# Eight products of a retention kernel issued as transpositions, and the first up stage in another order

## The chip, the cores and the metric

The kernel runs on one core of one Trainium2 chip. The time is the device time of one execution, in microseconds (us). The core has a matrix engine (TensorE; PE in the profile, its weight loads PEld), VectorE (DVE), ScalarE (ACT), GpSimd (POOL), and SyncE (SP), which here only issues DMAs. Each engine takes its instructions in the order of the program and stops at the first one whose inputs are not there.

## The reference, cut to what matters

```python
batch, n_heads, seq, head_dim = (4, 8, 768, 64)
for t in range(S):                      # retention, per batch and head
    state = gamma * state + outer(k[t], v[t])
    y[t] = scale * q[t] @ state
x = y.transpose(0, 2, 1, 3).reshape(3072, 512)
n_tokens, d_model, d_ff = (3072, 512, 1536)
g = x @ w_gate                          # feed-forward (SwiGLU)
out = (g * sigmoid(g) * (x @ w_val)) @ w_out
```

The weights arrive as 64-bit floats, q, k and v as 32-bit floats.

## The kernel before, in words

The 3072 tokens are worked through in four segments of 768 tokens, each of six chunks of 128 tokens (three chunks of two batches). A segment has an up stage (products with w_gate and w_val, for 12 blocks f of 128 columns of d_ff) and a down stage (products with w_out). Retention is computed chunk by chunk with a mask of decays inside a chunk and a state carried between chunks. Only the first segment's up stage is touched by the change. It is special in two ways: retention of its own six chunks precedes the products, and the weights are read raw from DRAM, turned to 32-bit floats on ScalarE, VectorE and GpSimd, and written back to DRAM for the later segments.

To keep the precision of 32-bit floats in a fast one-pass format, x and the weights are each split into three parts (a, b, c). A product of a weight block with 384 tokens is 12 matmuls in one bank of PSUM: four each for the parts a, b and c, in this order.

**What sets the order.** The order of nearly all work is a list written out by hand, PLAN (lines 51 to 229). Each token of it calls one step (the table at lines 576 to 597); the order of the tokens is the order of instructions on every engine, and of DMAs on SyncE's queue. A token is a letter and a number n, after a colon a part. The ones that the texts below use:

- Loads, all on SyncE's queue: `A` one of five pieces of the decay tables (A0: half the mask, A1 and A2: the other half, A3: q's decays, A4: k's decays). `ln:w` one operand of chunk n: w = 0 k (laid out with the head dimension on the partitions), 1 q, 2 v, 3 k's second layout (tokens on the partitions). `Un:b`, `Vn:b` the raw weights of block n into raw buffer b (512 KB for w_val and as much for w_gate; for the first block the two halves are loaded separately). `Zn` writes converted weights back to DRAM. Blocks 12 to 17 are the six pairs of rows of w_out.
- Retention of chunk n: `s` scores (matmuls L632, then two VectorE multiplications with the mask, L638). `r` makes k's second layout for chunks 0 and 1, which have no load `l0:3`, `l1:3`: four products on TensorE of 128 columns of k with a unit matrix (L693), left in a bank of PSUM. `K0` and `E1` scale that result by the decays (VectorE L653; ScalarE L660, eight instructions), `k`, `q`, `Q` scale k and q (GpSimd or VectorE). `t` the chunk's contribution to the state (L715), all in bank 6, then added or copied out (ScalarE L718 for chunks 0 and 1, VectorE L720 later). `g` decays the state (ScalarE L701). `o` the part of y from the old state (L730), `m` the part from the scores (L744) and the first part of x (ScalarE L1000). `x` the other two parts of x.
- Conversion of weight block n: `a`, `b`, `c` on ScalarE (L533, L536, L539), `S` on VectorE (L546), `C` on VectorE (L554) or GpSimd (L556, for the first two blocks and for w_out). `T` forms sums of weight blocks for later segments. `c` of block f stands behind the load of block f + 2 into the same raw buffer and waits for it to land.
- Products: `nf:0`, `nf:1`, `nf:2` make the three parts of the w_gate block f on ScalarE (L991), VectorE (L994) and GpSimd (L997); `nf:3` to `nf:5` do so for w_val. `p` and `v` are the products of blocks 0 and 1 for a third of the tokens (L937), `G` and `W` those of the later blocks for half the tokens (L919; G with w_gate, W with w_val). `u`/`i` apply SiLU on ScalarE (L943, L443), `y`/`j` multiply on VectorE (L948, L443). Each of the four banks is used again for the next block: `G` of block f + 1 waits for `i` of block f, `W` for `j`.

The function that the diff touches is `rows_of`; `scale_k` and `scale_k_act` read its result, `state` reads theirs.

Of the kernel before, what the change touches and what calls it, by code (L numbers as in the profile page):

```python
# [17 lines left out]
P = 128  # L18
# [7 lines left out]
L = 3  # L26
# [22 lines left out]


PLAN = """
    A0 l0:0 l1:0 A2 A1 U0:0 I0 l0:2 s0 a0:1 s1 A3 b0:1 c0:1 r0 l2:1 l2:0 A4 S0:1 m0 r1 l2:3 l1:2 K0
    l3:0 s2 l3:1 Q2 V0:0 E1 x0:2 C0:1 n0:0 t0 l2:2 m1 t1 l4:1 a0:0 b0:0 n0:1 s3 S0:0 x0:1 x1:1 c0:0
    k2 l4:0 U1:1 q3 g2 n0:2 o2 C0:0 n0:3 l3:3 o3 g3 a1:1 b1:1 m2 x1:2 l3:2 t2 n0:4 s4 a1:0 l5:0 S1:1
    n0:5 l5:1 b1:0 p0:0 u0:0 l4:2 l5:2 x2:1 v0:0 k3 q4 S1:0 m3 c1:1 t3 s5 y0:0 U2:0 x3:2 q5 x2:2
    c1:0 x3:1 o4 m4 C1:1 T0:0 U12:3 o5 n1:0 C1:0 x4:1 n1:1 m5 p0:1 x5:1 a2 v0:1 n1:3 T0:1 n1:2 u0:1
    b2 n1:4 U3:1 p1:0 h0 T1:0 p1:1 T0:2 y0:1 S2 U4:0 l5:3 a12 x5:2 T1:1 n1:5 u1:0 a3 x4:2 v1:0 Z0
    v1:1 p0:2 y1:0 u1:1 y1:1 c2 C2 v0:2 p1:2 b12 u0:2 v1:2 T1:2 U5:1 n2:0 a4 b3 Z1 n2:1 n2:3 y0:2 S3
    c3 n2:4 n2:2 C3 U6:0 G2:0 u1:2 y1:2 G2:1 T2:0 i2:0 n3:0 S12 n2:5 W2:0 b4 n3:1 W2:1 T2:1 S4 i2:1
    l4:3 U13:2 n3:3 c12 n3:2 T2:2 a5 c4 G3:1 C4 j2:0 c13 n3:4 j2:1 b5 G3:0 U7:1 i3:0 C12 n4:0 Z2  # L60
    n4:3 T3:0 n3:5 Z12 n4:1 S5 W3:0 n4:4 i3:1 c5 a6 n4:2 T3:1 n4:5 a13 W3:1 G4:0 G4:1 C5 b6 n5:0
    j3:1 T4:0 T3:2 T4:1 W4:1 U14:3 n5:3 j3:0 i4:1 n5:1 U8:0 b13 g4 n5:4 S6 W4:0 T4:2 n5:2 c6 Z3 L
    j4:1 i4:0 T5:0 a7 S13 G5:1 C6 n5:5 n6:0 Z4 j4:0 C13 b7 G5:0 n6:1 U9:1 W5:1 n6:3 i5:0 i5:1 c14 S7
    T5:1 T5:2 a8 n6:2 Z5 n6:4 T6:0 W5:0 G6:1 c7 C7 Z13 j5:0 n7:0 n6:5 G6:0 j5:1 b8 W6:1 i6:1 n7:3
    n7:1 U10:0 k4 a14 U15:2 k5 T6:1 n7:2 b14 n7:4 G7:1 S8 i6:0 c8 g5 T6:2 a9 T7:0 S14 W6:0 C8 i7:1
    G7:0 c15 i7:0 j6:1 Z6 T7:1 T7:2 U11:1 j6:0 n8:0 n7:5 n8:3 n8:1 n8:4 C14 n8:2 b9 W7:1 j7:1 Z14 S9
    a10 h1 W7:0 n8:5 c9 G8:0 C9 j7:0 a15 i8:0 Z7 b15 G8:1 n9:0 a11 U16:3 T8:0 S15 n9:1 P1 b10 W8:0
    n9:3 W8:1 S10 c10 t4 C15 n9:2 n9:4 C10 c16 G9:0 i8:1 T9:0 n9:5 Z15 b11 a16 i9:0 G9:1 j8:1 U17:2
    S11 t5 T9:1 n10:0 W9:1 h2 j8:0 b16 n10:1 T8:1 S16 W9:0 i9:1 T8:2 P0 n10:3 j9:1 n10:2 C16 G10:0
    j9:0 n10:4 P2 c11 i10:0 1/was0.0 G10:1 Z16 C11 n10:5 T10:0 T9:2 Z8 0/h0.0 n11:0 0/h0.1 W10:0  # L70
    n11:3 a17 n11:4 W10:1 1/sc0 T11:0 T11:1 Z9 i10:1 0/W0 1/begin n11:1 T11:2 Z11 0/h0.2 n11:2 b17
# [236 lines left out]
T0, UP0 = 30.0, 8.35  # L308
# [61 lines left out]
def tile_retnet_swiglu(  # L370
# [13 lines left out]
    nc = tc.nc  # L384
# [89 lines left out]
    T3, B22, B12, T1, B21, B11, T2, T4 = 0, 1, 2, 2, 3, 4, 5, 6  # L474
# [87 lines left out]
    def sums_t(piece, parts=range(3)):  # L562
# [16 lines left out]
        "g": lambda n: decay(cs[n]), "t": lambda n: state(cs[n]),  # L579
        "E": lambda n: scale_k_act(cs[n]),  # L580
        "r": lambda n: rows_of(n), "I": lambda n: unit_of(), "B": lambda n: small_tables(),
        "R": lambda n: decay_rows(), "D": lambda n: spread_rows(), "F": lambda n: keep_rows(),
        "k": lambda n: scale_k(cs[n]), "q": lambda n: scale_q(cs[n]),
# [36 lines left out]
    def pairs(t):  # L620
        return t.rearrange("p (n t) -> p n t", n=NP)
# [41 lines left out]
    unit = loads[:, ds(10 * 512, P)]  # L663
# [24 lines left out]
    def rows_of(n):  # L688

        c = cs[n]  # L690
        kt, t = pairs(chunks[c][0]), banks[2 + n]
        for m in range(NP):
            nc.tensor.matmul(t[:, ts(m, P)], kt[:, m], unit, start=(m == 0), stop=True,  # L693
                             skip_group_check=True)
        chunks[c][3], turned[c] = early[4 * n + 3], t

    def decay(c):
# [581 lines left out]
    t = down_stage(0, end)  # L1279
    for s in range(1, NSEG):  # L1280
# [8 lines left out]
        t = down_stage(s, t)  # L1289
# [50 lines left out]
```

## Time and profile before

| | us |
|---|---|
| time, median of 3 runs | 644.33 (644.0 to 646.4) |
| time of the profiled execution | 643.53 |
| its span, first to last instruction | 641.5 |
| TensorE busy | 634.0 |
| VectorE, ScalarE, GpSimd busy | 485.3, 393.9, 269.1 |

The time of an execution is about 2.0 us longer than the span. A line of the timeline gives the start, the duration, the engine, the line of the kernel, the operation, the tiles that it writes and reads, how often it was merged, and in brackets how long the engine stood idle before it and for what. A float32 matmul of the retention part shows as two records, one of the x-parts as one. Retention of the first segment lies between 5.8 and 30.5 us, the products of blocks 0 and 1 between 20.7 and 45.1 us, those of blocks 2 to 11 from 45.0 to 132.4 us (with small pieces of retention between), then the first down stage begins.

### The profile page before, as it was taken

What the parts mean: (1) busy time and instruction counts of PE and PEld (TensorE: products, weight loads), DVE (VectorE), ACT (ScalarE), POOL (GpSimd) and SP (SyncE); (2) the same over time, 40 slices, a digit from 0 to 9 for tenths busy, and PEclk for the clock granted to TensorE, in tenths of its full rate; (3) what the DMA queues carried; (4) which work ended last, traced back from release to release, by engine and by line L of the source; (5) the groups of instructions that cost most, each with busy time, mean ns of one, the idle gap of its engine ahead of it and who ended that gap; (6) DMA issues with size and microseconds to landing.
All of it is one profiled execution on the core that took longest, in us unless ns stands there. A gap on an engine that the chain in (4) does not pass through costs nothing.

```text
span 641.5 us, 14166 instructions
## 1 busy us (share of the span) xinstructions
PE 634.0 (99%) x5595; PEld 581.7 (91%) x5595; DVE 485.3 (76%) x710; ACT 393.9 (61%) x868; POOL 269.1 (42%) x177
## 2 busy tenths in 40 slices
PE   8999999999999999999999999999999999999997
PEld 7999998988779999997778999998777999999886
DVE  4879787998898887665787869675789866768351
ACT  4778888677865555566766555564785555655221
POOL 2635553644427865630002665550101666663000
PEclk9999999999999999999999999999999999999999
DMA  9999888789887445258775640457777444304554
GB/s 319 345 334 324 321 299 304 260 283 306 298 277 290 173 149 173 74 173 270 242 239 214 198 159 13 182 198 240 230 241 259 159 163 172 117 1 150 190 189 177
DMA packets 50626, 139.60 MB, mean 218 GB/s; under 512 B 5120, under 2 KB 18176, under 8 KB 50560
## 3 DMA queue, kind: packets, MB, share of 16 engines
q1 hardware_dynamic: 49984, 137.92, 62.5%
q8 instruction: 44, 0.72, 0.4%
q10 hardware_dynamic: 576, 0.79, 0.3%
q14 instruction: 22, 0.18, 0.1%
HBM read 108.80 MB, written 29.88 MB: 216 GB/s over the span
## 4 chain that ended last, share of the span: by engine, by line
PE 85%; DMA 8%; ACT 4%; DVE 2%; issue 1%; SPq 0%; ACTq 0%
PE bank L1088 41%; PE bank L1157 31%; PE bank L789 6%; PE bank L919 4%; DMA rawp<-in_w_gate_dram 3%; DMA wup<-loads 1%; DMA oitem<-wdnt 1%; PE bank L744 1%; DMA wdn<-first 1%; DMA hT<-in_v_n_dram 1%; ACT first L533 1%; PE bank L632 1%; ACT bank L536 1%; PE bank L730 1%; DMA hT<-in_q_t_dram 1%
## 5 line engine op out<-in xcount | busy, mean ns | idle before, releaser
L1157 PE MATMUL bank<-oitem,gitem 128*128 128x512 f32 x867 | 208.2, 394 | 0.4 <-DMA oitem<-wdnt 0.4
L1157 PEld LDWEIGHTS bank<-oitem,gitem 128*128 128x128 f32 x867 | 159.7, 188 | 34.8 <-DMA oitem<-wdnt 0.8
L997 POOL TENSOR_TENSOR gitem<-gitem 128x768 fp32r<-128x768 f32 x72 | 142.0, 1982 | 114.4 <-DVE gitem L994 97.4
L1088 PE MATMUL bank<-xa,gitem 128*128 128x384 f32 x864 | 160.5, 334 | 0.0
L1088 PEld LDWEIGHTS bank<-xa,gitem 128*128 128x128 f32 x864 | 150.8, 188 | 0.2
L997 POOL TENSOR_TENSOR oitem<-oitem 128x256 fp32r<-128x256 f32 (+1 forms) x60 | 65.1, 1092 | 52.0 <-DVE oitem L994 43.6
L919 PE MATMUL bank<-xa,oitem 128*128 128x384 f32 x480 | 84.7, 335 | 0.8 <-ACT tmp L443 0.7
L1088 PE MATMUL bank<-xb,gitem 128*128 128x384 f32 x432 | 84.5, 334 | 0.0
L994 DVE SCALAR_TENSOR_TENSOR gitem<-gitem,loads 128x768 fp32r<-128x768 f32 x72 | 77.2, 1087 | 9.6 <-ACT gitem L991 8.0
L919 PEld LDWEIGHTS bank<-xa,oitem 128*128 128x128 f32 x480 | 83.0, 188 | 1.6 <-ACT tmp L443 1.4
L1088 PEld LDWEIGHTS bank<-xb,gitem 128*128 128x128 f32 x432 | 75.9, 188 | 0.4
L991 ACT ACTIVATE gitem<-loads 128x768 fp32r<-128x768 f32 x72 | 59.6, 842 | 25.8 <-PE bank L1088 16.7
L994 DVE SCALAR_TENSOR_TENSOR gitem<-gitem,hT 128x768 fp32r<-128x768 f32 x48 | 49.4, 1032 | 25.7 <-ACT gitem L991 25.7
L991 ACT ACTIVATE gitem<-hT 128x768 fp32r<-128x768 f32 x48 | 40.1, 841 | 34.6 <-PE bank L1157 31.1
L1022 ACT COPY chunk_x<-bank 64x128 f32<-64x128 f32 x144 | 36.6, 260 | 30.5 <-PE bank L789 20.4
L400 DVE SCALAR_TENSOR_TENSOR gitem<-gitem 128x768 fp32r<-128x768 f32 x48 | 48.7, 1022 | 0.9
L816 POOL TENSOR_TENSOR loads<-loads,tab 128x512 f32<-128x512 f32 x9 | 14.0, 1556 | 82.2 <-PE bank L789 58.7
L1088 PE MATMUL bank<-xb,oitem 128*128 128x384 f32 x216 | 43.4, 335 | 0.0
L1088 PEld LDWEIGHTS bank<-xb,oitem 128*128 128x128 f32 x216 | 38.0, 188 | 0.3
L1105 DVE TENSOR_TENSOR hT<-bank,tmp 128x384 f32<-128x384 f32 x36 | 19.9, 554 | 20.2 <-PE bank L1088 19.9
L994 DVE SCALAR_TENSOR_TENSOR oitem<-oitem,loads 128x256 fp32r<-128x256 f32 (+1 forms) x42 | 33.7, 807 | 1.4 <-ACT oitem L991 1.3
L1103 ACT COPY tmp<-bank 128x384 f32<-128x384 f32 x36 | 17.2, 477 | 27.4 <-PE bank L1088 18.4
(118 smaller groups left out, 790.5 us busy)
## 6 DMA issues: line engine op xcount, KB each, us to landing
loads<-wup SPq DMA_DIRECT2D x36, 896.0 KB, 4.8
oitem<-wdnt SPq DMA_DIRECT2D x33, 768.0 KB, 4.3
wdnt<-oitem SPq DMA_DIRECT2D x12, 768.0 KB, 6.2
wup<-first SPq DMA_DIRECT2D x9, 896.0 KB, 5.7
rawp<-in_w_gate_dram SPq DMA_DIRECT2D x12, 512.0 KB, 6.6
rawp<-in_w_val_dram SPq DMA_DIRECT2D x12, 512.0 KB, 5.6
rawp<-in_w_out_dram SPq DMA_DIRECT2D x12, 512.0 KB, 7.6
out_dram<-chunk_x SPq DMA_DIRECT2D x21, 256.0 KB, 2.2
```

The costliest lines, as they stand in the source:

```text
L400: stt(o, x, 1.0, y, op0=mul, op1=op)
L789: nc.tensor.matmul(o, a, b, start=start, stop=True, skip_group_check=True)
L816: (pool if i else both)(t, t, qdec, op=mul)
L919: nc.tensor.matmul(o, w[:, a, ts(b, P)], X0[:, a, i, NC - 1 - b], start=a == b == 0, stop=a == 2 and b == NC - 1, skip_group_check=True)
L991: act(o[0], x, AF.Copy, scale=CUT / FAR)
L994: stt(o[1], f32(o[0]), -FAR, x, op0=mul, op1=add)
L997: op(o[2], f32(o[0]), f32(o[1]), op=add)
L1022: copy(cx[half[i], ds(2 * h, 2), c, half[z]], y.rearrange("p (b t) -> p b t", b=2))
L1088: nc.tensor.matmul(o, w[:, a, k], x[:, a, KH - 1 - k], start=start and a == k == 0, stop=a == 2 and k == KH - 1, skip_group_check=True)
L1103: steps = (lambda: copy(p1, x), lambda: tt(c11, z, p1, op=add), lambda: act(gate, c11, AF.Silu, scale=ONE), lambda: copy(u2, x), lambda: c ...
L1105: lambda: copy(p5, wb), lambda: tt(h1, x, p5, op=add),
L1157: nc.tensor.matmul(banks[tok][:, cols], hs[f][:, a, ds(i * TH + u * P, P)], wo[f][:, a, cols], start=f == a == 0, stop=f == NF - 1 and a = ...
```

## The change

Two edits. In `rows_of` the four products with the unit matrix are issued by TensorE's transposition call instead of as matmuls. In PLAN the first 17 lines (367 tokens) are the same tokens in another order; the rest of PLAN is unchanged. On TensorE the order of the tokens changes only here: r1 goes ahead of m0 and r0 behind it; m2 moves between o2 and o3, and m3 ahead of t2; p0:1 moves ahead of s5 and t3 behind s5; some pairs of G and of W for the same block are exchanged. On SyncE's queue A2 goes ahead of l0:0, A3 moves behind l1:2, l2:3 behind V0:0, l2:2 ahead of V0:0, l3:2 ahead of l4:1, l3:3 behind l5:0, U4:0 ahead of U3:1, l4:3 much later, Z13 and U15:2 ahead of Z5 and U10:0.

```diff
 PLAN = """
-    A0 l0:0 l1:0 A2 A1 U0:0 I0 l0:2 s0 a0:1 s1 A3 b0:1 c0:1 r0 l2:1 l2:0 A4 S0:1 m0 r1 l2:3 l1:2 K0
-    l3:0 s2 l3:1 Q2 V0:0 E1 x0:2 C0:1 n0:0 t0 l2:2 m1 t1 l4:1 a0:0 b0:0 n0:1 s3 S0:0 x0:1 x1:1 c0:0
-    k2 l4:0 U1:1 q3 g2 n0:2 o2 C0:0 n0:3 l3:3 o3 g3 a1:1 b1:1 m2 x1:2 l3:2 t2 n0:4 s4 a1:0 l5:0 S1:1
-    n0:5 l5:1 b1:0 p0:0 u0:0 l4:2 l5:2 x2:1 v0:0 k3 q4 S1:0 m3 c1:1 t3 s5 y0:0 U2:0 x3:2 q5 x2:2
-    c1:0 x3:1 o4 m4 C1:1 T0:0 U12:3 o5 n1:0 C1:0 x4:1 n1:1 m5 p0:1 x5:1 a2 v0:1 n1:3 T0:1 n1:2 u0:1
-    b2 n1:4 U3:1 p1:0 h0 T1:0 p1:1 T0:2 y0:1 S2 U4:0 l5:3 a12 x5:2 T1:1 n1:5 u1:0 a3 x4:2 v1:0 Z0
-    v1:1 p0:2 y1:0 u1:1 y1:1 c2 C2 v0:2 p1:2 b12 u0:2 v1:2 T1:2 U5:1 n2:0 a4 b3 Z1 n2:1 n2:3 y0:2 S3
-    c3 n2:4 n2:2 C3 U6:0 G2:0 u1:2 y1:2 G2:1 T2:0 i2:0 n3:0 S12 n2:5 W2:0 b4 n3:1 W2:1 T2:1 S4 i2:1
-    l4:3 U13:2 n3:3 c12 n3:2 T2:2 a5 c4 G3:1 C4 j2:0 c13 n3:4 j2:1 b5 G3:0 U7:1 i3:0 C12 n4:0 Z2
-    n4:3 T3:0 n3:5 Z12 n4:1 S5 W3:0 n4:4 i3:1 c5 a6 n4:2 T3:1 n4:5 a13 W3:1 G4:0 G4:1 C5 b6 n5:0
-    j3:1 T4:0 T3:2 T4:1 W4:1 U14:3 n5:3 j3:0 i4:1 n5:1 U8:0 b13 g4 n5:4 S6 W4:0 T4:2 n5:2 c6 Z3 L
-    j4:1 i4:0 T5:0 a7 S13 G5:1 C6 n5:5 n6:0 Z4 j4:0 C13 b7 G5:0 n6:1 U9:1 W5:1 n6:3 i5:0 i5:1 c14 S7
-    T5:1 T5:2 a8 n6:2 Z5 n6:4 T6:0 W5:0 G6:1 c7 C7 Z13 j5:0 n7:0 n6:5 G6:0 j5:1 b8 W6:1 i6:1 n7:3
-    n7:1 U10:0 k4 a14 U15:2 k5 T6:1 n7:2 b14 n7:4 G7:1 S8 i6:0 c8 g5 T6:2 a9 T7:0 S14 W6:0 C8 i7:1
-    G7:0 c15 i7:0 j6:1 Z6 T7:1 T7:2 U11:1 j6:0 n8:0 n7:5 n8:3 n8:1 n8:4 C14 n8:2 b9 W7:1 j7:1 Z14 S9
-    a10 h1 W7:0 n8:5 c9 G8:0 C9 j7:0 a15 i8:0 Z7 b15 G8:1 n9:0 a11 U16:3 T8:0 S15 n9:1 P1 b10 W8:0
-    n9:3 W8:1 S10 c10 t4 C15 n9:2 n9:4 C10 c16 G9:0 i8:1 T9:0 n9:5 Z15 b11 a16 i9:0 G9:1 j8:1 U17:2
+    A0 A2 l0:0 I0 l1:0 A1 U0:0 s0 a0:1 s1 c0:1 b0:1 l0:2 S0:1 l2:1 r1 m0 A4 r0 C0:1 K0 x0:2 l2:0 E1
+    n0:0 l3:0 l1:2 s2 A3 Q2 t0 n0:1 l3:1 l2:2 m1 V0:0 l2:3 h0 a0:0 l3:2 t1 b0:0 s3 o2 q3 x1:1 c0:0
+    k2 l4:1 S0:0 l4:0 x0:1 C0:0 m2 U1:1 n0:2 x2:2 n0:3 l5:0 x1:2 x2:1 n0:4 o3 l3:3 m3 x3:2 g2 a1:0
+    a1:1 n0:5 t2 l5:1 x3:1 c1:1 b1:1 s4 S1:1 p0:0 l4:2 b1:0 q4 u0:0 k3 v0:0 g3 C1:1 p0:1 S1:0 c1:0
+    n1:0 s5 U2:0 u0:1 a2 q5 C1:0 t3 y0:0 n1:3 T0:0 T0:1 l5:2 o4 n1:1 n1:4 m4 U12:3 o5 n1:2 m5 b2
+    x4:2 v0:1 T1:0 n1:5 p1:0 a12 p1:1 S2 T0:2 y0:1 U4:0 v1:0 v1:1 u1:0 u1:1 x5:1 y1:0 U3:1 c2 l5:3
+    x4:1 x5:2 p0:2 a3 C2 Z0 v0:2 T1:1 n2:0 n2:3 u0:2 y1:1 T1:2 n2:1 n2:2 p1:2 v1:2 u1:2 U5:1 Z1 a4
+    b3 U6:0 y0:2 b12 n2:4 y1:2 n2:5 S3 T2:0 G2:0 c3 C3 T2:1 G2:1 i2:1 T2:2 n3:0 i2:0 n3:1 k5 W2:0 b4
+    S4 U13:2 n3:3 W2:1 n3:4 a5 j2:0 c4 n3:2 g4 j2:1 C4 n4:0 c12 Z2 n4:1 G3:1 S12 n3:5 G3:0 U7:1 n4:2
+    i3:0 W3:0 C12 b5 Z12 i3:1 n4:3 a6 W3:1 h1 S5 n4:4 T3:0 G4:0 G4:1 j3:1 c5 C5 j3:0 i4:0 U8:0 T3:1
+    T4:0 g5 T3:2 c13 U14:3 T4:1 n4:5 i4:1 T4:2 Z3 l4:3 W4:1 n5:0 b6 n5:1 j4:1 W4:0 a13 S6 n5:2 n5:3
+    b13 n5:4 c6 a7 S13 G5:1 C6 n5:5 j4:0 G5:0 W5:0 n6:0 c14 i5:0 T5:0 i5:1 T5:1 C13 L b7 n6:1 T5:2
+    Z4 n6:3 U9:1 j5:0 S7 Z13 W5:1 n6:4 c7 n6:2 T6:0 j5:1 U15:2 Z5 a8 C7 n6:5 G6:0 U10:0 G6:1 i6:0
+    W6:1 n7:0 n7:1 a14 n7:3 W6:0 i6:1 b8 b14 T6:1 j6:1 n7:4 n7:2 n7:5 T6:2 S8 c15 G7:1 Z6 S14 a9
+    i7:1 k4 c8 G7:0 U11:1 W7:1 T7:0 j6:0 C8 i7:0 n8:0 n8:3 C14 T7:1 n8:1 b9 Z14 n8:2 W7:0 a10 S9 c9
+    a15 T7:2 j7:0 b15 n8:4 n8:5 j7:1 C9 Z7 S15 n9:0 C15 G8:1 n9:1 G8:0 W8:1 b10 i8:1 n9:3 n9:2 W8:0
+    i8:0 S10 t4 c10 G9:0 n9:4 U16:3 C10 T8:0 n9:5 T9:0 P1 c16 a11 Z15 b11 a16 i9:0 G9:1 j8:1 U17:2
     S11 t5 T9:1 n10:0 W9:1 h2 j8:0 b16 n10:1 T8:1 S16 W9:0 i9:1 T8:2 P0 n10:3 j9:1 n10:2 C16 G10:0
...
         for m in range(NP):
-            nc.tensor.matmul(t[:, ts(m, P)], kt[:, m], unit, start=(m == 0), stop=True,
-                             skip_group_check=True)
+            nc.tensor.transpose(t[:, ts(m, P)], kt[:, m], unit)
```

## The prediction

> **What bounds the kernel now.** First the page: busy time by engine.
>
> ```profile
> PE 634.0 (99%) x5595; PEld 581.7 (91%) x5595; DVE 485.3 (76%) x710; ACT 393.9 (61%) x868; POOL 269.1 (42%) x177
> ```
>
> TensorE has 641.5 - 634.0 = 7.5 us without work in the whole span. No reordering can gain more than what stands idle in the part it touches, so I looked next at who TensorE waited for (total us, times, longest):
>
> ```profile
> PE bank L632 <- DMA hT<-in_k_t_dram: 1.0, 1, 1.0
> PE bank L919 <- ACT tmp L443: 0.7, 1, 0.7
> PE bank L744 <- DMA hT<-in_v_n_dram: 0.6, 1, 0.6
> ```
>
> The first and third are waits for first loads, which stay. The busy time by stretches places the second (TensorE, weight loads, VectorE, ScalarE, GpSimd, clock, DMA share, GB/s):
>
> ```profile
> 80.00:90.00 10.00, 10.00 (x59) 10.00 (x58) 8.71 (x13) 7.60 (x14) 5.89 (x5) 1.00 1.00 339
> 90.00:100.00 10.00, 9.32 (x55) 9.03 (x54) 6.64 (x11) 8.78 (x13) 3.47 (x3) 1.00 0.84 301
> ```
>
> From 15 to 98 us TensorE is full, while the other engines have room. "Full" holds for the rate too: 72 matmuls of 384 columns take 12.68 us in the chain, 0.176 us each, and so do 312 in 54.25 us. So what counts is (1) TensorE's own work, (2) the few holes, (3) new holes. The timeline of the start:
>
> ```profile
> 9.76 1.09 PE L744 MATMUL bank<-tmp,hT 128*64 128x128 f32 x16 [0.64 <-DMA hT<-in_v_n_dram]
> ...
> 10.78 1.16 PE L693 MATMUL bank<-loads,hT 128*128 128x128 f32 x8
> ...
> 11.98 1.74 ACT L660 ACTIVATE hT<-bank,tab 128x64 f32<-128x64 f32 x8 [0.49 <-PE bank L693]
> ...
> 14.08 0.42 ACT L718 COPY states<-bank 128x256 f32<-128x256 f32 x1
> ...
> 14.56 0.69 PE L715 MATMUL bank<-hT 128*64 128x64 f32 x16
> ```
>
> Read here: one chunk's r is eight records in 1.09 us to the next step, 0.136 each; and t1 (14.56) stands behind ScalarE's copy of t0 out of bank 6, at the end of E1 (1.74), n0:0 and the copy.
>
> **The transpositions.** They replace 2 x 4 products. r0 was at 7.96 in the shadow of the wait for v; r1 was on the path. In the new order r1 goes into that shadow and r0 onto the path behind m0. The trace has no transposition. If each product stays two records, nothing changes (1.09). If each becomes one record of the same pace, a chunk takes 4 x 0.136 = 0.55. If four run one after the other without overlap at the longest record of L693 (0.377), they take 1.5, 0.4 more than now. I take 0.55, since the same operands at the nearest row run at that pace: r0 ends at 10.85 + 0.55 = 11.4, -0.54 on TensorE.
> [...]
> But little of it arrives. E1 can start when m0's first part of x is done (11.49): 11.5 + 1.74 + 0.63 (n0:0) + 0.42 (copy) = 14.3, for all three run in this order on ScalarE. GpSimd's C0:1, which n0:0 needs, comes 0.7 later (b0:1 moves behind c0:1, 0.67), to 11.8 + 1.3 = 13.1, still ahead of E1's end. t1 is at 14.35 instead of 14.56: **-0.2**. Bounds -0.5 and +0.4.
>
> **The loads at the start.** A2 ahead of l0:0: 128 KB at 376 GB/s, 0.35. s0 starts at 6.2; with s1 (together 2.13) and r1 (0.55) TensorE is at 8.9, still ahead of m0, whose v lands at 9.62 behind the same bytes as before. So nothing; without that cover 0.35. A3 moves back by four loads of 0.68, to 13.1; Q2 needs it at 14.3 and q3 at 13.8. A4 gets earlier.
> From t1 the new order runs s3, o2, m2, o3, m3, t2, s4 (steps of 1.09, 0.95, 1.02, 0.95, 1.02, 0.46, 1.09): 14.35 + 0.65 + 6.58 = 21.6 for p0:0, which was at 20.74 with m3 (1.02) still to come, so 21.76. Inputs: v of chunk 2 had landed at 17.99; four places earlier it lands near 14.5, needed at 17.0. v of chunk 3 takes the place that landed at 18.67; needed at 19.0. k's second layout of chunk 2 takes the place of 17.99, so GpSimd runs k2 to 19.1, then C0:0 (1.30) to 20.4, n0:2 (1.28) to 21.7; p0:0 needs n0:2 for its third part, after eight matmuls of 0.12, at 22.6. n0:5 is there at 23.4 and v0:0 needs it at 24.0. t2's 19.8 needs k2 at 19.1. Margins of 0.3 to 0.9 us: cost 0, price under rivals.
>
> **Blocks 2 and 3.** ScalarE stands idle 13.4 us in all for raw w_gate (the rows that read rawp), as c of block f waits for the load of block f + 2. Putting U4:0 ahead of U3:1 lands U4 at about 36.4 instead of 40.0 and U3 at 39.4 instead of 36.65 (U4 can issue behind a2, about 30.8; 4.3 to the first landing as at 29.43; 1.5 for each of four transfers). For block 3: a3 to 40.6, U5:1 issued there, landed by 48.2 (7.6 as before), c3 1.15, C3 1.22, n3:0 0.63, n3:1 0.68, n3:2 1.35: 53.2. G3:1 needs it for its third part at 53.28 - 0.2 + 1.4 = 54.5. Covered by 1.3; before, n3:2 was done at 53.08, as late. Then blocks 4 to 8 have more margin than before where it was small: W3:0 (n3:5, 0.55 us), G5:0 (i4:0, 0.43), W6:1 (j5:1, 0.48) and W7:1 (j6:1, 0.43) all get their step ahead of a blocking one.
>
> **The hole at 99 us.** The timeline:
>
> ```profile
> 96.90 1.12 ACT L539 ACTIVATE first<-rawp 128x1024 int32<-128x1024 uint32 x1 [0.89 <-DMA rawp<-in_w_gate_dram]
> 98.05 1.23 DVE L554 CUSTOM_DVE_ANT_0 first<-bank,first 128x2048 uint16<-128x2048 uint16 x1 [2.25 <-ACT first L539]
> 98.33 1.15 ACT L533 ACTIVATE first<-rawp 128x1024 f32<-128x1024 f32 x1 [0.32 <-DMA wdn<-first]
> 99.19 0.55 DVE L443 TENSOR_TENSOR hT<-bank,tmp 128x384 f32<-128x384 f32 x1
> ...
> 99.89 4.40 PE L919 MATMUL bank<-xa,oitem 128*128 128x384 f32 x24 [0.68 <-ACT tmp L443]
> ...
> 104.52 1.29 POOL L997 TENSOR_TENSOR oitem<-oitem 128x512 fp32r<-128x512 f32 x1
> ```
>
> The page blames ScalarE, but j7:0 (99.19, VectorE) ended at 99.74, and it stood behind C9, which waited for c9, which waited for U11:1. In the new order both j7:0 and j7:1 stand ahead of C9: this hole of 0.68 goes. A second one, about 0.3 at 107 (G9:1 behind i8:1, which stands behind c10 and c16), goes too, since i8:1 and i8:0 now stand ahead of c10. Together -1.0. What is late next is the last row: n9:2 on GpSimd (104.52 to 105.81), the end of a chain from Z14's landing (98.23): a15, b15, S15, C15 (2.81), n9:2. G9:0, at 104.83, needed it at 106.2, a margin of 0.4. TensorE 1.2 earlier needs it 0.8 earlier. U11:1, in front of Z14 on the queue, waits for a9; a9 now stands ahead of c8, so it issues about 1 us earlier (its own 90.60 was just behind a9's 90.57), and Z14 lands up to 1 us earlier. I credit **-0.7** of the 1.0; bounds -1.0 and 0.
> Behind 107 us the chain of waits is TensorE's rows alone to 145 us, so what is gained there stays.
>
> **Sum.** -0.2 - 0.7 = -0.9: the profiled execution's 643.53 becomes 642.6. The median of the runs is 0.8 above it, so the forecast on the median is 644.33 - 0.9 = **643.4**. Half a per cent is 3.2 us, about what a measurement of this kernel can tell from no change.
>
> **Rivals.**
> Given back: the chain to n9:2 does not get earlier (or the transpositions remain two records each and the chain moves half way). For it: margin of 0.4 in a chain behind a store. Then only 0.2 to 0.4 is left: 644.1.
> GpSimd early: l2:3 or V0:0 lands 1.4 late (l2:2 took 2.04 where its neighbours took 0.68), k2 holds C0:0, and v0:0 waits 0.8 to 1.5: 643.4 + 1.1 = 644.5.
> Half clock: the 16 records of the warm-up (L1253) take 0.213 each, those of L693 with the same shape 0.126 or less, so TensorE starts at about half its later rate. If r1 and the longer idle time ahead of m0 (0.9 instead of 0.64) threw it back for as long as the warm-up lasted (3.5 us), 1.8 us would be lost: 643.4 + 1.8 = 645.2. Against it: the 1.0 us idle ahead of s0 did not. [...]
> **Slower:** U3:1 behind U4:0. Its place is raw buffer 1, which C1:0 on GpSimd frees (29.40 before, about 30 now, behind k3, q4, q5 that wait for loads). It decides from the point where U3 lands later than 39.4 + 1.3 = 40.7. C1:0 later by 2.4 (the longest wait GpSimd had there), and U3 and U5 each at the longest landing of a raw load (9.2 instead of 7.6), are 5.6; less 1.3, TensorE stands 4.3 us, and later odd blocks follow: 644.33 + 4.3 = 648.6.
> All of it: both terms at their best, -0.5 - 1.0: 644.33 - 1.5 = 642.8.
>
> **Chances.** Forecast 0.38; given back 0.25; GpSimd early 0.08; half clock 0.05; all of it 0.04; slower 0.17; a gain that no row shows 0.03. Within 0.5%: 0.80; faster by more 0.03; slower by more 0.17. The range goes from all of it (642.8, less 0.3 for the spread of the runs below their median, once for before and once for after: 642.2) to the smaller half of the slower rival, 644.33 + 2.2 = 646.5, which is also where the slowest run of before lies; outside are the rest of that rival and the 0.03.
>
> **What would show it.** TensorE's instructions 5595 to 5587, and L693 as x8 at 0.55 us or less a chunk; t1 at 14.3; no idle time of L919 for ScalarE at 99; n9:2 ending ahead of 105.2. Wrong would be a TensorE wait between 20 and 60 us, above all at G3:1 (53 us), a wait for n9:2 longer than 0.5, or L1253's pace in L632 behind 10 us.

## The result, and the profile after

The changed kernel takes 646.61 us in the median of 14 runs (645.19 to 648.13), beside 644.88 for the kernel before on the same chip (14 runs, 642.98 to 647.74). The ratio is 1.0026, with a 95% interval from 1.0014 to 1.0038: slower by a quarter of a per cent, where a gain of 0.9 us was forecast. The profiled execution spans 644.1 us instead of 641.5. The page of the changed kernel, engines busy:

```profile
PE 634.3 (98%) x5587; PEld 580.2 (90%) x5587; DVE 484.4 (75%) x710; ACT 393.8 (61%) x868; POOL 269.5 (42%) x177
```

TensorE has eight matmuls and eight loads less, as worked out. What it waits for has changed (total us, times, longest):

```profile
PE bank L632 <- DMA hT<-in_k_t_dram: 1.6, 1, 1.6
PE bank L1156 <- DVE tmp L811: 1.1, 1, 1.1
...
PE bank L743 <- DMA hT<-in_v_n_dram: 1.0, 1, 1.0
PE bank L918 <- ACT tmp L443: 0.5, 1, 0.5
```

The second line is new: a wait of 1.1 us for VectorE, in the down stage, whose plan was not touched. (The rewritten function is a line shorter, so the lines of before from 694 on stand one lower here.) The busy time by stretches of the changed kernel, columns as before:

```profile
80.00:90.00 10.00, 9.48 (x55) 9.03 (x54) 7.14 (x12) 7.68 (x11) 4.33 (x3) 1.00 1.04 373
90.00:100.00 10.00, 9.95 (x57) 9.63 (x56) 7.84 (x14) 8.51 (x11) 5.68 (x5) 1.00 0.81 296
...
130.00:140.00 10.00, 8.80 (x114) 6.80 (x114) 9.90 (x12) 7.78 (x24) 6.23 (x4) 1.00 0.65 238
```

and the last stretch in the kernel before:

```profile
130.00:140.00 10.00, 10.00 (x156) 8.40 (x158) 9.90 (x13) 7.68 (x22) 5.33 (x4) 1.00 0.73 237
```

The hole of 0.68 left the stretch from 90 to 100 and one of 0.52 came between 80 and 90. Set matmul against matmul, counted from the end of both programs, TensorE is 0.02 us behind the kernel before at 123 us (the up stage as a whole gained and lost nothing), 1.27 behind at 133, 1.42 at 140, 2.1 at 290 and 2.6 at the end. So half of the profile's loss comes within a few microseconds around 133 us.

**The chain to that hole.** The timeline of the changed kernel, lines of that chain alone:

```profile
123.03 0.32 SPq L1132 DMA_DIRECT2D oitem<-wdn  x1
...
127.89 0.64 ACT L999 ACTIVATE oitem<-oitem 128x512 fp32r<-128x512 f32 x1 [5.08 <-DMA oitem<-wdn]
...
129.93 0.70 DVE L1006 SCALAR_TENSOR_TENSOR oitem<-oitem 128x512 fp32r<-128x512 f32 x1 [2.01 <-POOL oitem L1002]
...
133.64 0.68 DVE L811 TENSOR_TENSOR tmp<-bank,local 128x512 f32<-128x512 f32 x1
...
134.37 1.65 PE L1156 MATMUL bank<-oitem,gitem 128*128 128x512 f32 x6 [1.09 <-DVE tmp L811]
```

and the same lines of the kernel before:

```profile
123.01 0.32 SPq L1133 DMA_DIRECT2D oitem<-wdn  x1
...
125.75 0.63 ACT L1000 ACTIVATE oitem<-oitem 128x512 fp32r<-128x512 f32 x1 [3.16 <-DMA oitem<-wdn]
...
127.80 0.69 DVE L1007 SCALAR_TENSOR_TENSOR oitem<-oitem 128x512 fp32r<-128x512 f32 x1 [0.70 <-POOL oitem L1003]
...
131.51 0.68 DVE L812 TENSOR_TENSOR tmp<-bank,local 128x512 f32<-128x512 f32 x1
```

Read it from the load. (A token with a slash belongs to a segment: 0/W0 loads the first block of w_out for the down stage of segment 0, 0/d0.0 to 0/d0.2 make its three parts, and 1/dec0.0 puts the mask on scores of the next segment.) W0, 256 KB, is issued at the same moment in both (123.0). It lands at 125.65 in one and 127.78 in the other. ScalarE starts on it at once (0/d0.0), GpSimd and VectorE follow (L1006, 0/d0.2), and 1/dec0.0 (L811), which stands behind 0/d0.2 on VectorE, frees a bank of PSUM that TensorE needs. In the kernel before it ends at 132.2, 0.9 ahead of the fourth matmul with w_out (at 133.10), which needs that bank; 2.1 later it holds TensorE for 1.1. The question became why one load takes 2.64 us and the other 4.75.

### The profile page after: what moved, and what is told of

The parts are those of the page before. It is cut to its first block, busy times and chain, and to the rows that moved or that the text cites. A ratio compares the mean times of both kernels' runs of the same rounds, so it can differ in the third digit from the quotient of the medians.

```text
span 644.1 us, 14154 instructions
## 1 busy us (share of the span) xinstructions
PE 634.3 (98%) x5587; PEld 580.2 (90%) x5587; DVE 484.4 (75%) x710; ACT 393.8 (61%) x868; POOL 269.5 (42%) x177
## 4 chain that ended last, share of the span: by engine, by line
PE 80%; DMA 11%; DVE 3%; ACT 3%; issue 2%; SPq 1%; POOL 0%; ACTq 0%; DVEq 0%
PE bank L1087 40%; PE bank L1156 27%; PE bank L788 5%; DMA wdnt<-oitem 3%; PE bank L936 3%; PE bank L918 2%; DMA wup<-loads 1%; DMA rawp<-in_w_out_dram 1%; DMA oitem<-wdnt 1%; DMA loads<-in_q_t_dram 1%; PE bank L743 1%; DMA rawp<-in_w_gate_dram 1%; DMA hT<-in_v_n_dram 1%; DMA wdn<-first 1%; PE bank L632 1%
```

## The experiments

The kernels ran in three groups (e1 to e4; f1 to f4; g1 to g3 and e7), each on one chip, beside runs of the kernel before on that chip. Most medians are of 12 runs, that of g1 of 6, those of the kernel before of 29 or 35. Ratios are to the kernel before, with 95% intervals; each profile is of one execution. "Idle at 133" is the time that TensorE's matmuls between 132 and 136 us are late against the tightest sequence of the same matmuls in any of the profiles.

### First: which of the two edits, and which wait

The transpositions alone, in the old order (e1):

```diff
-            nc.tensor.matmul(t[:, ts(m, P)], kt[:, m], unit, start=(m == 0), stop=True,
-                             skip_group_check=True)
+            nc.tensor.transpose(t[:, ts(m, P)], kt[:, m], unit)
```

> The kernel before with the transpositions alone, its order untouched. By my account of the first 20 us: a chunk's four products take 0.5 to 0.6 us instead of 1.09; r0 lies in the wait for v and saves nothing; r1's 0.5 is hidden at t1 behind ScalarE's copy of t0 (14.5 us). So 0.0 to 0.2 us faster than before, too little to measure, and TensorE's later holes (99 and 107 us) as before. If transpositions disturb TensorE's pace or its later work, the loss of the whole change (1.7 us) or part of it is here: 645.5 or more.

Measured: 646.41 (before: 645.15), ratio 1.0019 [1.0001, 1.0038].

The new order alone, that is the changed kernel with the matmuls back (e2):

```diff
-            nc.tensor.transpose(t[:, ts(m, P)], kt[:, m], unit)
+            nc.tensor.matmul(t[:, ts(m, P)], kt[:, m], unit, start=(m == 0), stop=True,
+                             skip_group_check=True)
```

> The kernel after with the products as matmuls again: the new order alone. If the order holds the whole loss: within 0.5 us of after (646.6), with the holes at 87 us (0.7) and at 133 us (1.3) in the same places. If the transpositions hold it: back to before, 644.9.

Measured: 645.44, ratio 0.9996 [0.9977, 1.0014]. Both edits, but the first pair of rows of w_out converted and loaded where it was before (e3):

```diff
- i2:0 n3:1 k5 W2:0 b4 S4 U13:2 n3:3 W2:1 n3:4 a5 j2:0 c4 n3:2 g4 j2:1 C4 n4:0 c12 Z2
- n4:1 G3:1 S12 n3:5 G3:0 U7:1 n4:2 i3:0 W3:0 C12 b5 Z12 i3:1
+ i2:0 S12 n3:1 k5 W2:0 b4 S4 U13:2 n3:3 c12 W2:1 n3:4 a5 j2:0 c4 n3:2 C12 g4 j2:1 C4 n4:0 Z2
+ n4:1 G3:1 n3:5 G3:0 Z12 U7:1 n4:2 i3:0 W3:0 b5 i3:1
...
- U8:0 T3:1 T4:0 g5 T3:2 c13 U14:3
+ U14:3 U8:0 T3:1 T4:0 g5 T3:2 c13
```

> The kernel after with the conversion of w_out's first pair put back to where it stood before: S12 ahead of n3:1, c12 behind n3:3, C12 behind n3:2, Z12 ahead of U7:1, U14:3 ahead of U8:0. Theory 1 (the late first pair): U14:3's 1 MB no longer stands just ahead of Z3 on the queue, Z3 lands at about 72.5 instead of 74.9, so a7, U9:1 and c7 come 2 us earlier, the hole at 87 us goes, Z7 issues before 96 instead of 98.3, and the hole at 133 us shrinks to less than 0.5: 1.2 to 2 us faster than after, 644.6 to 645.4. Theory 2 (U3:1 behind U4:0): no change, 646.6, holes at 87 and 133 stay.

Measured: 646.2, ratio 1.0023 [1.0005, 1.0042]. Both edits, with 1/dec0.0 ahead of the step that waits for W0 on VectorE (e4):

```diff
- 0/d0.1 i11:1 0/d0.2 0/h1.1 i11:0 1/l5 C17 1/q0.1 0/W1 0/h2.0 W11:1 1/dec0.0 T10:1
+ 0/d0.1 i11:1 1/dec0.0 0/d0.2 0/h1.1 i11:0 1/l5 C17 1/q0.1 0/W1 0/h2.0 W11:1 T10:1
```

> The kernel after with one VectorE step of the next segment, 1/dec0.0 (the mask on the scores that lie in bank 4), ahead of 0/d0.2, which waits for w_out's first block. Theory 1: the hole at 133 us (1.3) is D0.4 waiting for bank 4, held by dec0.0, which stands in VectorE's order behind the step that waits for W0's landing (127.8). Moved ahead, dec0.0 ends by 129 and the hole goes, though W0 lands as late as in after: 0.9 to 1.4 us faster than after, about 645.4. Rival (D0's own operands are late, or the queue is behind as a whole): the hole stays or moves to the next product, less than 0.3 us gained.

Measured: 646.64, ratio 1.0024 [1.0005, 1.0042].

As far as these four go, the loss comes with the eight transpositions, in either order of the plan, and the new order is worth nothing that can be measured. Undoing the later w_out pair did not help. Taking 1/dec0.0 out of the queue removed its wait and made another of the same size, for the next step on VectorE; e4's TensorE:

```profile
132.66 2.25 PE L1150 MATMUL bank<-oitem,gitem 128*128 128x512 f32 x9
135.83 0.51 PE L1150 MATMUL bank<-oitem,gitem 128*128 128x512 f32 x1 [0.93 <-DVE hT L437]
```

So 1/dec0.0 was only the first to pass the delay on; that W0's landing is its source is borne out further on, where idle time and landing go together over fourteen profiles. With the matmuls kept (e2) the idle time at 133 is 0.44; with the transpositions it is 1.37 (e1), 1.52, 1.58 (e3), 1.09 (e4).

### Second: the transpositions, or sixteen instructions less?

How can products at 11 us delay a load at 123? The trace's DMA records offer a way. A queue of the kind "instruction" (q8) brings 44 packets of 16 KB, 0.72 MB in all. The trace does not name the engine whose code they are; that it is TensorE's is read from their spacing. In the kernel before, a packet starts every 7.7 us from 137.40 to 183.71, where TensorE starts 15.7 matmuls a microsecond, and every 21.8 us from 202.83 to 268.33, where TensorE starts 5.8: 121 and 126 matmuls from one packet to the next. In windows around the load, the kernel before (packets, MB, share of the 16 engines), from 123.0 to 124.1 us:

```profile
q1 hardware_dynamic: 20, 0.04, 14.8%
q8 instruction: 1, 0.02, 5.7%
```

and the changed kernel, from 124.3 to 126.3:

```profile
q1 hardware_dynamic: 194, 0.71, 91.2%
q8 instruction: 1, 0.02, 5.8%
```

In the first window q1 keeps the 16 engines 15% busy, with 0.04 MB. In the changed kernel it keeps them 98.5% busy, with the end of the store ahead of W0 in it, from W0's issue to 124.36. That store is an obvious suspect, but it is not needed: in e1 the engines are 6.2% busy for the 0.9 us behind W0's issue, and W0 still takes 4.60. A packet of code is under way beside W0 in both: before, from 123.02 to 124.02, starting with W0's issue; after, from 124.36 to 126.23, 1.3 us behind it and, at 1.87 us beside 1.00, nearly twice as long, among the packets of the stores and loads that follow W0 on the queue. And 44 packets for 11,190 loads and matmuls are 254 of these each in the mean, so with sixteen instructions less the later packets may be fetched at another place in the work. The theory of the places: not the transposition but the count of instructions decides.

Four kernels part the two. Four small matmuls of zeros behind the warm-up, whose result nobody reads, give the sixteen instructions back; they are added to the transpositions alone (f1), to the kernel before (f2) and to the changed kernel (f3):

```diff
     warm_up(8)
+    for _ in range(4):
+        nc.tensor.matmul(banks[3][:32, :32], warm[:, :32], warm[:, :32], start=True, stop=True,
+                         skip_group_check=True)
```

> The kernel before with the transpositions alone, and four more small float32 matmuls of zeros (32 x 32) behind the warm-up, whose output nobody reads: TensorE's count of instructions is 5595 again. Theory (places of the instruction fetches: with 16 fewer instructions, loads and matmuls together, every later fetch of TensorE's code falls on another instruction): the ratio goes back to 1.000, some 645.1, and no idle time of 1.1 us at 133 us nor of 0.27 at 492. Rival (the transpositions themselves cost it, by the clock or by their result in the bank): the ratio stays at 1.002, some 646.4.

> The kernel before, with its matmuls, and the same four small matmuls of zeros behind the warm-up: 5603 records of each kind on TensorE. Theory (places of the fetches): the fetches fall 16 instructions earlier in the work than before; the time may move by up to 1.5 us either way, and where it does, it does so in the same places (133, 183, 492 us). Rival (the transpositions themselves): 1.000, as before, since the matmuls end ahead of the first load's landing.

> The changed kernel with the same four small matmuls of zeros behind the warm-up: as many TensorE instructions as with the matmuls. Theory (places of the fetches): the time of the new order with matmuls, ratio 1.000, some 645.2, and the idle time of 1.26 us at 133 falls below 0.5. Rival (the transpositions themselves): 1.0025, some 646.6, with the idle time there.

The fourth has the matmuls, and sixteen instructions less in the warm-up:

```diff
-            nc.tensor.matmul(banks[3][:, :P], warm[:, :P], warm[:, :P], start=True, stop=True,
+            nc.tensor.matmul(banks[3][:, :2 * P], warm[:, :P], last[:, :2 * P], start=True, stop=True,
...
+    nc.vector.memset(last[:, :2 * P], 0.0)
-    warm_up(8)
+    warm_up(4)
```

> The kernel before, with its matmuls, and a warm-up of four matmuls of 256 columns in place of eight of 128 (zeros; nobody reads the result): as long, but 16 instructions fewer, as with the transpositions. Theory (places of the fetches): it loses what the transpositions alone lose, ratio 1.002, some 646.4, with idle time of about 1.1 us at 133 and 0.3 at 492. Rival (the transpositions themselves): 1.000, some 645.1.

Measured, beside 644.78: f1 644.38, 1.0001 [0.9979, 1.0023]; f2 644.99, 0.9992 [0.9971, 1.0014]; f3 644.99, 0.9999 [0.9981, 1.0018]; f4 645.85, 1.0017 [0.9998, 1.0035]. f1, f3 and f4 came out on the side of the places; f2 parts nothing, since both sides allowed 1.000. Transpositions with the count restored cost nothing, and their TensorE runs through at 133 (f1):

```profile
129.80 1.37 PE L913 MATMUL bank<-xa,oitem 128*128 128x384 f32 x7
131.01 3.60 PE L1151 MATMUL bank<-oitem,gitem 128*128 128x512 f32 x15
```

while the old code with sixteen instructions less has the late load and the wait (f4; ScalarE, then TensorE):

```profile
127.60 0.63 ACT L1000 ACTIVATE oitem<-oitem 128x512 fp32r<-128x512 f32 x1 [4.49 <-DMA oitem<-wdn]
...
134.11 2.26 PE L1157 MATMUL bank<-oitem,gitem 128*128 128x512 f32 x7 [0.32 <-DVE tmp L812]
```

The f4 row is not as sharp as expected: its interval just reaches 1.000, and its idle time at 133 is 0.76, not 1.1.

### Third: the fetch itself, or the store behind the load?

> The changed kernel; the store of 896 KB and the q load that follow W0's load on the queue (Z11, 1/l5) stand behind the next load of that kind (0/W1). In ten profiles so far W0's load landed 1.5 to 1.7 us after the instruction fetch at its side had ended. Theory (the fetch itself holds the load): W0 still lands 1.5 to 1.7 after the fetch's end, and the idle time at 133 us stays above 0.8 if the fetch lies as late as in the changed kernel. Rival (the store behind it shares the engines, and the fetch only decides how soon the store is issued): W0 lands 2.6 us or less after its issue, whatever the fetch does, and the idle time falls below 0.3; ratio then 1.001 or less, unless the late q load costs it again.

```diff
- n11:1 T11:2 Z11 0/h0.2 n11:2 b17 j10:0 0/d0.0 j10:1 0/h1.0 S17 G11:0 c17 n11:5 G11:1 W11:0 0/d0.1 i11:1
- 0/d0.2 0/h1.1 i11:0 1/l5 C17 1/q0.1 0/W1 0/h2.0
+ n11:1 T11:2 0/h0.2 n11:2 b17 j10:0 0/d0.0 j10:1 0/h1.0 S17 G11:0 c17 n11:5 G11:1 W11:0 0/d0.1 i11:1
+ 0/d0.2 0/h1.1 i11:0 C17 1/q0.1 0/W1 Z11 1/l5 0/h2.0
```

Measured: 650.8 (before: 644.78), ratio 1.0112 [1.0084, 1.0141]. New holes from 138 us on cost more than all else here (the late q load, most likely), so the time says nothing on the question. The trace does. W0 is alone on the queue, and still its reader on ScalarE starts at 127.41:

```profile
122.81 5.78 SPq L1126 DMA_DIRECT2D oitem<-wdn  x2
...
127.41 0.63 ACT L993 ACTIVATE oitem<-oitem 128x512 fp32r<-128x512 f32 x1 [5.01 <-DMA oitem<-wdn]
```

The fetch lasted from 123.92 to 125.80, W0 landed at 127.30, 1.50 behind its end, and TensorE stood for 1.25 at 133. The store that follows is not needed for it; the rival falls.

With nothing behind W0 on the queue, its packets can be followed one by one: 128 of 2 KB, and sixteen of 4 bytes. By 124.95, 120 of the first kind and fifteen of the second have started. From then to 125.77, with the code's packet still under way, none starts:

```profile
DMA packets 0, 0.00 MB, mean 0 GB/s; under 512 B 0, under 2 KB 0, under 8 KB 0
```

and from 125.77 to the landing at 127.30 the rest:

```profile
DMA packets 9, 0.02 MB, mean 11 GB/s; under 512 B 1, under 2 KB 1, under 8 KB 9
```

The first of the nine starts at 125.78, as the code's packet ends, the last, of 4 bytes, at 126.88. So one sixteenth of the load stood still until the code had passed. f4 has the same mark: fifteen of its sixteen 4-byte packets start by 126.11, the last at 126.99, and W0 lands at 127.50.

Two more shifts, by replacing some of the warm-up's eight matmuls (g2 keeps four and adds twenty small ones, g3 keeps six and adds ten):

```diff
-    warm_up(8)
+    warm_up(4)
+    for _ in range(20):
+        nc.tensor.matmul(banks[3][:32, :32], warm[:, :32], warm[:, :32], start=True, stop=True,
+                         skip_group_check=True)
```

> The changed kernel; of the warm-up's eight matmuls of zeros four stay, and twenty of 32 x 32 take the place of the others: about as long, and 64 TensorE instructions more than in the changed kernel. Theory (places of the fetches): the fetch near 124 us falls earlier in the work, ends ahead of W0's issue plus 1.2, W0 lands less than 3.3 us after its issue, and the idle time at 133 is below 0.3; the ratio goes to 1.000 give or take 0.001, since the other fetches move too. Rival (the transpositions themselves): 1.0025.

> The same with six full matmuls and ten of 32 x 32: 32 TensorE instructions more than in the changed kernel. Theory: as with 64, W0's landing follows the end of the fetch by 1.5 to 1.7 us, and the idle time at 133 is below 0.4; ratio 1.000 give or take 0.001. Rival: 1.0025.

Measured: g2 645.98, 1.0021 [1.0003, 1.0039]; g3 645.03, 1.0004 [0.9987, 1.0022]. g3 is as expected. In g2 the fetch is over before W0 is issued, W0 takes 3.11 us, and there is no idle time at 133:

```profile
131.20 3.84 PE L1156 MATMUL bank<-oitem,gitem 128*128 128x512 f32 x15
```

but it lost as much elsewhere, which was not expected. Its profile has three holes of 0.4 to 0.6 between 155 and 161 us, where no other kernel has one above 0.3, and one of 1.8 at 177 that others have too (f2, f3 and f4: 1.0 to 2.0). Whether a fetch stands behind these was not tried.

The fourteen profiles together, ordered by how far the fetch starts behind W0's issue (us; landing counted from W0's issue, then from the fetch's end):

| kernel | TensorE instructions | fetch behind issue | it took | landing | after the fetch | idle at 133 | ratio |
|---|---|---|---|---|---|---|---|
| g2 | 5619 | -1.42 | 0.95 | 3.11 | 3.58 | 0 | 1.0021 |
| before | 5595 | 0.01 | 1.00 | 2.64 | 1.63 | 0 | 1 |
| f1 | 5595 | 0.08 | 0.95 | 2.73 | 1.70 | 0 | 1.0001 |
| e7 | 5595 | 0.40 | 1.15 | 3.11 | 1.56 | 0 | 1.0008 |
| f2 | 5603 | 0.57 | 0.96 | 3.04 | 1.51 | 0 | 0.9992 |
| g3 | 5603 | 0.70 | 0.96 | 3.18 | 1.52 | 0 | 1.0004 |
| f3 | 5595 | 0.71 | 1.01 | 3.28 | 1.56 | 0.18 | 0.9999 |
| e1 | 5587 | 0.89 | 2.17 | 4.60 | 1.54 | 1.37 | 1.0019 |
| e2 | 5595 | 1.00 | 1.13 | 3.64 | 1.51 | 0.44 | 0.9996 |
| g1 | 5587 | 1.11 | 1.88 | 4.49 | 1.50 | 1.25 | 1.0112 |
| after | 5587 | 1.33 | 1.87 | 4.75 | 1.55 | 1.52 | 1.0026 |
| e3 | 5587 | 1.35 | 2.03 | 4.95 | 1.57 | 1.58 | 1.0023 |
| f4 | 5587 | 1.41 | 0.88 | 3.96 | 1.67 | 0.76 | 1.0017 |
| e4 | 5587 | 1.65 | 1.06 | 4.19 | 1.48 | 1.09 | 1.0024 |

In thirteen of them W0 lands 1.48 to 1.70 us after the fetch has ended, whatever the order, the products or the queue behind it. A landing of 3.3 us or less behind the issue costs nothing or nearly so; above 3.9 TensorE stands.

How the count sets the place of a fetch is not a plain shift. At 0.176 each, eight matmuls and their loads would be 1.4 us, and f4's fetch is 1.40 later than that of before; but that is chance, for TensorE runs 64 small matmuls in 1.16 us just there, and f2, with sixteen instructions more, has its fetch not earlier but 0.56 later. Count the matmuls still to come when a fetch begins. For the one beside W0 they are 4567 to 4571 in the six kernels of 5587, 4570 to 4627 in the five of 5595, 4588 and 4579 in the two of 5603. Two fetches later they are 4345 to 4355 in all fourteen. For one between 483 and 493 us they are 852 or 853 in the six and 940 to 948 in the other eight, and near 492 five of the six (all but g1) stand for 0.35 to 0.39, where before, f1, f3, e2, e7 and g3 do not stand at all (f2 and g2 do, for 0.55 and 0.89). So the count does move fetches, at some places by far more than itself and at others not at all; what fixes the places is left open.

### The credit of 0.7: does a hole that goes stay gained?

The kernel before, with j7:0 and i8:1 where the new order has them against C9 and c10:

```diff
- c9 G8:0 C9 j7:0 a15 i8:0 Z7
+ c9 G8:0 j7:0 C9 a15 i8:0 Z7
...
- S10 c10 t4 C15 n9:2 n9:4 C10 c16 G9:0 i8:1 T9:0
+ S10 i8:1 c10 t4 C15 n9:2 n9:4 C10 c16 G9:0 T9:0
```

> The kernel before with j7:0 ahead of C9 and i8:1 ahead of c10, as the new order has them, and nothing else. The prediction's step (a hole that goes at 99 and 107 us stays gained): no idle time there, and 0.7 us less, ratio 0.9989. Rival (the stretch up to 110 us is as long as its loads of w_gate and w_val, so that TensorE's idle time only moves): 1.000, with idle time of about 0.7 elsewhere between 85 and 130 us. Second rival (that idle time is there in some executions only): it is absent in the profile, and the ratio is 1.000.

Measured: 644.72 (before: 644.78), ratio 1.0008 [0.9992, 1.0024]. The hole at 99 us is gone, and there is one of 0.61 at 93 instead, and short ones of 0.18 at 60 and 0.17 at 108:

```profile
93.08 2.20 PE L914 MATMUL bank<-xa,oitem 128*128 128x384 f32 x11 [0.61 <-DVE hT L438]
```

The holes of 45 to 125 us are not a property of the order either: the profiles of e1 and f1, with the old order, have none above 0.15, nor have those of f3, g2 and g3, with the new order; the others have 0.5 to 1.4 us of them in varying places. What makes them come and go is left open.

## Why the prediction was wrong, point by point

**The size of the transpositions was right.** They became one record instead of two, four to a chunk:

```profile
10.11 1.09 PE L743 MATMUL bank<-tmp,hT 128*64 128x128 f32 x16 [0.97 <-DMA hT<-in_v_n_dram]
...
11.13 0.65 PE L693 MATMUL bank<-loads,hT 128*128 128x128 f32 x4
...
11.72 1.16 PE L632 MATMUL bank<-hT 64*128 64x128 f32 x16
...
11.73 1.75 ACT L660 ACTIVATE hT<-bank,tab 128x64 f32<-128x64 f32 x8
...
14.31 0.69 PE L714 MATMUL bank<-hT 128*64 128x64 f32 x16
```

From the start of r0 to the next step are 0.59 us (0.55 worked out, 1.09 before); E1 starts 0.25 earlier and t1 at 14.31 (14.3 worked out). In the old order the way from s0 to p0:0 took 14.91 us with the matmuls (before and f4) and 14.72 with the transpositions (f1), which fits the gain of 0.2; e1 (14.74), e7 (15.82) and f2 (16.05) do not compare, because their first scores ran slower (see half clock below).

**The step that failed** is the sentence that behind 107 us "the chain of waits is TensorE's rows alone to 145 us, so what is gained there stays", together with the pricing of the transpositions by their own duration alone: -0.2 in the sum, where e1 measured 646.41 against 645.15, +1.3. The sum had no term for what sixteen instructions less do to the later fetches. The chain names what ended last, not what nearly did. W0's landing passed through three engines to a bank that came free 0.9 us before TensorE needed it, and when W0 landed went by the place of an instruction fetch. With sixteen instructions less that fetch began 0.89 to 1.65 us behind W0's issue, in the kernels of 5595 at 0.01 to 1.00. What would have shown it beforehand is TensorE's code queue in a window around each load that lands just ahead of its use; the profile of before had the 44 packets. The five kernels of 5587 TensorE instructions whose queue was left alone lie at 1.0017 to 1.0026, mean 1.0022; the six others of 5595 and 5603 at 0.9992 to 1.0008, mean 1.0000. The difference is 1.4 us; the idle time at 133 is 1.26 in the mean of those five and 0.1 or so in the others. That it is the count, and not the transposition, is shown by f1, f3 and f4 together; by each interval alone it would not be. That the fetch holds the load up is shown by its position in thirteen profiles and by the packets of g1, where a sixteenth of the load waits for the code's packet to end; that both sat on one DMA engine was not shown, for the trace names no engine. Not every loss runs through 133 us: g2 and the profile of f2 lost elsewhere.

**The credit of -0.7** failed in the way of the rival "given back", by another chain than the one named. The hole at 99 went, as forecast (j7:0 at 98.19 and j7:1 at 99.26, both ahead of C9):

```profile
98.19 0.55 DVE L443 TENSOR_TENSOR hT<-bank,tmp 128x384 f32<-128x384 f32 x1
...
99.26 0.55 DVE L443 TENSOR_TENSOR hT<-bank,tmp 128x384 f32<-128x384 f32 x1
...
99.72 1.22 DVE L554 CUSTOM_DVE_ANT_0 first<-bank,first 128x2048 uint16<-128x2048 uint16 x1
...
104.97 1.31 POOL L996 TENSOR_TENSOR oitem<-oitem 128x512 fp32r<-128x512 f32 x1
```

But n9:2 ended at 106.28, not ahead of 105.2: Z14, which was to land up to 1 us earlier, was issued at 94.17 instead of 91.62 and landed at 98.32 instead of 98.23, and a15 then stood behind c9 to 99.03 (98.33 before). And a hole of 0.52 was there at 86.9 already, since U9:1's w_gate landed at 82.21 (78.49 before) and i6:1 ended at 87.37 behind the step that waits for it. e7 shows the same without any of the rest: the hole goes, another comes, the time stays.

**Loads at the start**: A2 ahead of l0:0 was taken as covered. s0 started at 6.50, not 6.2, and m0 at 10.11 instead of 9.76, so of the 0.2 only 0.1 was left at p0:0 (21.67 against the 21.76 worked out for the old order with m3), and nothing at the end of block 1 (45.02 against 44.96).

**Blocks 2 and 3** held: n3:2 ended at 54.03 (53.2 worked out) and no TensorE wait lies between 20 and 60 us, so the slower rival (U3:1 behind U4:0) did not come, nor GpSimd early. **Half clock** did not come in the changed kernel: the granted clock was 1.00 from 0 to 20 us, and the 32 records of its first scores took 2.06. But the rival was a real one. In seven of the fourteen profiles, with transpositions (e1, e4, f3, g3) and without (e2, e7, f2), these records took 3.0 to 3.8 us, ahead of the first r, and in the old order with matmuls p0:0 came 15.82 and 16.05 behind s0 there (e7 and f2) instead of 14.91. The granted clock shows it only in e1 (0.88 in the mean from 0 to 10 us, and 0.996 over the profiled execution, beside 0.999 or 1.000 in the others). e7 and the kernel before have the same TensorE steps there, so the slow pace is not a property of the order; what decides it is left open. **The range** ended 0.1 below the result, and its base, the 644.33 of three runs, was 0.55 below the 644.88 of fourteen; the way was wrong all the same. The change was given a chance of 0.80 to lie within half a per cent, which it does, but no case in it was a loss of 1 to 2 us that comes from anything but the steps themselves.

## What to carry to other kernels

Here, with the bounding engine 98% busy, an edit of a few tenths of a microsecond was smaller than what its count of instructions did: sixteen less moved the time by 0.2%, by transpositions or by a shorter warm-up alike, and sixteen more (f2) did not. So test such an edit a second time with the count restored by dummy instructions, before its loss or gain is put down to what it does. And read in the profile not only which wait ends last, but which loads land within a microsecond of their use, and what else is on the DMA engines then.

## What the runs showed of the hardware

A fetch of 16 KB on q8, read as TensorE's code, took 0.88 to 2.17 us at the place of W0's load, and this load of 256 KB landed 1.48 to 1.70 us after the fetch's end in thirteen of fourteen profiles, even when it had been issued 1.65 us before the fetch began; in g1 eight of its 128 packets started only as the code's packet ended. The first 32 records of float32 scores took 2.1 us in seven profiles and 3.0 to 3.8 in the other seven. A float32 transposition of 128 x 128 is one record where the product with a unit matrix is two, and four of them take 0.59 us to the next step instead of 1.09.
